# Issuing both transposes of a chunk ahead of their two copies

## The chip, the cores and the metric

The kernel runs on one core of a Trainium2 chip. The metric is the device time of one execution in microseconds (us); each kernel is run several times and the median is quoted. "Fast" runs are those in the chip's normal state, and only these are compared.

## The reference, cut to what matters

```python
# q, k, v: (8 batches, 8 heads, 576 positions, 64), float32
scores = scale * np.matmul(q, k.transpose(0, 1, 3, 2))
ret = scores * Dmat[None, :, :, :]            # causal, times gamma_h ** (i - j)
attn = np.matmul(ret, v)
x = attn.transpose(0, 2, 1, 3).reshape(4608, 512)
h = x @ w_in                                  # 512 -> 2048
g = h * np.tanh(softplus(h))                  # Mish
out = g @ w_out                               # 2048 -> 512
```

## The kernel before

The 4,608 rows are cut into chunks of 128, four chunks to a tile of 512. For each chunk, q and k are loaded, scaled by powers of gamma on VectorE (DVE), transposed on TensorE (PE) against an identity matrix into PSUM (the memory where this kernel's matmuls put their results), copied to SBUF (where it keeps its operands), and multiplied into scores. Masking and the product with v follow, then the two dense layers. The kernel fixes the order of PE's work by hand: pieces of attention for a later chunk are placed between groups of matmuls of the dense layers. A piece that waits holds back what stands behind it: in the prediction's timeline the 16 matmuls of L425, which need nothing from the transposes, start at 45.89, only after k's transposes, which had waited until 45.67.

The second tile (chunks 4 to 7) is transposed by `step_t`, the function that the change touches:

```python
def step_t(n):
    m, u = divmod(n, 2)
    qk = turned(m)                                              # SBUF tile "qkT" of a pair of chunks
    tp = ps_sc.tile([P, 4, NP, P], BF16, name="sc")             # PSUM; q in tp[:, 0], k in tp[:, 1]
    for i, copy in enumerate((nc.scalar.copy, nc.vector.tensor_copy)):
        flat = pairs[m]["qks"][:, i, u].rearrange("p h d -> p (h d)")
        for p in range(NP):                                     # NP = 4
            nc.tensor.transpose(tp[:, i, p, :], flat[:, ts(p, P)], ident)
        copy(qk[:, i, u], tp[:, i])
```

Around it stand the first dense layer with Mish on ScalarE (ACT), and the scores:

```python
def g1_chunk(n, f, nf=4):                                       # 16 matmuls of 128 columns
    ...
    nc.scalar.activation(gts[t][:, ds(f, nf), ts(s, P)], hp, AX.Mish)

def step_s(n):                                                  # needs both halves of qkT
    sc = ps_sc.tile([P, 2, NP, P], F32, name="sc")
    ... nc.tensor.matmul(sc[:, e, p, :], lhsT=qk[r, 1, u, p, :], rhs=qk[r, 0, u, p, :], ...)
    ... nc.vector.tensor_tensor(sm, sc, mask, op=OP.mult)

for n in range(4, 8):
    for fb in range(4):
        if n < 7:
            if fb == 0:
                one(n + 1, "T")                                 # step_t
            elif fb == 1:
                one(n + 1, "S")                                 # step_s
                ...
        g1_chunk(n, 4 * fb)
```

So from chunk 5 on one `g1_chunk` (16 matmuls) lies between a chunk's transposes and its scores. Chunk 4 is placed earlier, among the groups of the first tile, with two groups of four matmuls of 512 columns between.

## Time and profile before

| | before |
|---|---|
| median time | 321.31 us in the runs before the prediction, 321.19 with one more |
| PE busy | 305.4 us, 96% of the profiled span of 319.4 us |
| share of PE in the chain that ended last | 90% |
| PE idle before k's transposes, for ACT | 3.8 us, four times 0.94 |

A line of a timeline gives start and duration in us, engine, source line, operation, output and inputs, shapes and count, and in brackets the idle time of the engine before it with what ended that. PE's busy time contains a modelled pipeline tail after each last matmul (one short matmul is shown as 0.22 us though four in a row take 0.22), so an idle time in brackets is a little shorter than the hole in PE's stream. I therefore also use steps from one start to another. A view of a source line lists how long its engine sat idle before it and for whom.

### The profile page before, as it was taken

Reading aid. Unit: us, or ns where it says so; the run is one execution under the profiler, and the core shown is the slowest. Engines: PE = TensorE matmul, PEld = TensorE weight load, DVE = VectorE, ACT = ScalarE, POOL = GpSimd, SP = SyncE. Lnnn points to the kernel's source line nnn. Section 1 sums busy time; section 2 is a strip of 40 time slices with the busy share of each in tenths; the row PEclk is TensorE's granted clock in tenths of the full one; section 3 lists DMA queues with packets and bytes.
Section 4 is the critical chain, followed back from the end, with each engine's and each line's share of the span. In section 5 each row is a group of like instructions: output and inputs, shape, how many; then the busy total and the mean of one; then the engine's idle time right before and its main releaser. Section 6 shows DMA issues by size and latency. Waiting matters only on the chain.

```text
span 319.4 us, 6100 instructions
## 1 busy us (share of the span) xinstructions
PE 305.4 (96%) x2639; PEld 159.4 (50%) x2639; DVE 132.6 (42%) x178; ACT 129.6 (41%) x217; POOL 79.1 (25%) x102
## 2 busy tenths in 40 slices
PE   7788888999899999999999999999999999999995
PEld 2354477745555454444545454445454545444444
DVE  6733444047555675354444445353536232001111
ACT  5666566512464642243434343424242422333200
POOL 6687663551440040404131312140000000000000
PEclk9999999999999999999999999999999999999999
DMA  6999999999998549599795959595040400000032
GB/s 163 271 184 215 198 207 218 204 220 210 242 172 110 75 103 219 123 176 152 145 173 124 174 124 185 114 165 133 33 101 33 101 33 35 33 33 35 33 81 83
DMA packets 72474, 43.38 MB, mean 136 GB/s; under 512 B 55680, under 2 KB 63616, under 8 KB 72448
## 3 DMA queue, kind: packets, MB, share of 16 engines
q0 software_dynamic: 43952, 26.22, 55.8%
q1 hardware_dynamic: 28352, 16.65, 21.3%
q8 instruction: 20, 0.33, 0.5%
q10 hardware_dynamic: 144, 0.13, 0.1%
q14 instruction: 6, 0.05, 0.0%
HBM read 36.70 MB, written 9.44 MB: 144 GB/s over the span
## 4 chain that ended last, share of the span: by engine, by line
PE 90%; ACT 3%; SPq 2%; DMA 2%; DVE 1%; issue 1%; ACTq 0%; DVEq 0%
PE hp L402 34%; PE ops L440 32%; PE hp L440 6%; PE hp L425 5%; PE sc L338 3%; PE sc L387 2%; PE sc L380 2%; SPq L137 2%; PE st L359 2%; DMA kraw<-in_k_dram 2%; ACT qkT L310 1%; PE sc L309 1%; PE hp L452 1%; PE hp L413 1%; ACT qkT L297 1%
## 5 line engine op out<-in xcount | busy, mean ns | idle before, releaser
L402 PE MATMUL hp<-xT,w_in_t 128*128 128x512 bf16 x492 | 125.6, 380 | 0.5 <-ACT gT L427 0.5
L404 ACT ACTIVATE gT<-hp 128x512 bf16<-128x512 f32 x123 | 73.4, 597 | 128.6 <-PE hp L402 128.3
L440 PE MATMUL ops<-w_out_t,gT 128*128 128x512 bf16 x480 | 121.9, 379 | 0.0
L440 PEld LDWEIGHTS <-gT 128*128 128x128 bf16 x560 | 54.2, 98 | 64.7 <-issue 0.8
L460 DVE COPY res<-ops 128x512 f32<-128x512 f32 x30 | 20.7, 691 | 133.5 <-PE ops L440 133.5
L402 PEld LDWEIGHTS <-w_in_t 128*128 128x128 bf16 x492 | 45.6, 98 | 53.1 <-issue 0.8
L341 DVE TENSOR_TENSOR sm<-sc,mask 128x1024 bf16<-128x1024 f32 x36 | 42.6, 1217 | 13.6 <-PE sc L338 13.6
L318 POOL COPY seen<-qkT 1x1 bf16<-1x1 bf16 x10 | 1.8, 176 | 127.0 <-DMA qkT<-qks 127.0
L363 ACT ACTIVATE ssb<-st,diag 128x512 bf16<-128x512 f32 x32 | 20.2, 683 | 15.0 <-PE st L359 14.8
L107 POOL DMA_DIRECT2D qraw<-in_q_dram x16 | 17.2, 1074 | 24.7 <-DVE qks L280 18.5
L391 DVE CAST xT<-sc 128x512 bf16<-128x512 f32 x28 | 18.0, 685 | 4.7 <-PE sc L387 3.9
L280 DVE TENSOR_TENSOR qks<-kraw,gk 128x1024 bf16<-128x1024 f32 (+1 forms) x18 | 19.8, 1099 | 0.0
L280 DVE TENSOR_TENSOR qks<-qraw,gq 128x1024 bf16<-128x1024 f32 (+1 forms) x18 | 19.7, 1095 | 0.0
L440 PE MATMUL hp<-w_out_t,gT 128*128 128x512 bf16 x80 | 18.8, 380 | 0.0
L107 POOL DMA_DIRECT2D v<-in_v_dram x16 | 17.2, 1080 | 5.4 <-DMA kraw<-in_k_dram 2.7
L107 POOL DMA_DIRECT2D kraw<-in_k_dram x16 | 17.1, 1071 | 5.9 <-DVE qkT L297 3.7
L425 PE MATMUL hp<-xT,w_in_t 128*128 128x128 bf16 x276 | 17.1, 219 | 0.0
L425 PEld LDWEIGHTS <-w_in_t 128*128 128x128 bf16 x276 | 15.6, 98 | 0.7 <-issue 0.2
L387 PE MATMUL sc<-sm,v 128*64 128x128 bf16 x288 | 13.8, 220 | 0.6 <-DVE sm L341 0.6
L427 ACT ACTIVATE gT<-hp 128x512 bf16<-128x512 f32 (+1 forms) x18 | 10.3, 579 | 8.3 <-PE hp L425 8.1
L310 ACT COPY qkT<-sc 128x1024 bf16<-128x1024 bf16 x8 | 8.1, 1012 | 11.9 <-PE sc L309 11.9
L338 PEld LDWEIGHTS <-qkT 64*128 64x128 bf16 x288 | 8.1, 94 | 8.7 <-issue 6.4
(77 smaller groups left out, 163.2 us busy)
## 6 DMA issues: line engine op xcount, KB each, us to landing
out_dram<-res SPq DMA_DIRECT2D x31, 256.0 KB, 3.5
qraw<-in_q_dram POOLq DMA_DIRECT2D x12, 512.0 KB, 6.2
kraw<-in_k_dram POOLq DMA_DIRECT2D x12, 512.0 KB, 7.5
v<-in_v_dram POOLq DMA_DIRECT2D x12, 256.0 KB, 8.3
qraw<-in_q_dram POOLq DMA_DIRECT2D x8, 256.0 KB, 9.0
kraw<-in_k_dram POOLq DMA_DIRECT2D x8, 256.0 KB, 9.3
w_out_t<-in_moe_w_out_dram POOLq DMA_DIRECT2D x4, 512.0 KB, 12.1
w_in_t<-in_moe_w_in_dram POOLq DMA_DIRECT2D x6, 256.0 KB, 6.0
```

What stands on the lines that cost most here:

```text
L107: nc.gpsimd.dma_start(out=r[x][ds(off, ni)].rearrange("p u h d -> p (u h) d"), in_=src[ds(b, 2), :, ds(i0, ni), :].rearrange("b h p d -> p ...
L280: nc.vector.tensor_tensor(r["qks"][:, i, u], r["qk"[i]][:, u], g, op=OP.mult)
L338: nc.tensor.matmul(sc[:, e, p, :], lhsT=qk[r, 1, u, p, :], rhs=qk[r, 0, u, p, :], start=True, stop=True)
L341: nc.vector.tensor_tensor(sm.rearrange("p e n i -> p (e n) i"), sc.rearrange("p e n i -> p (e n) i"), (mask if len(chunks[n]) == 1 else ma ...
L363: nc.scalar.activation(ssb[:, :, :, e, :], st, AX.Copy, scale=diag[:, e:e + 1])
L387: nc.tensor.matmul(ot[ds(64 * e, 64), p, :], lhsT=vs[:, u, 2 * p + e, :], rhs=sm[:, e, p, :], start=(start and p == 0), stop=True, skip_gr ...
L391: (nc.scalar.copy if t < 2 else nc.vector.tensor_copy)(xts[t][:, :, ts(s, P)], ot)
L402: nc.tensor.matmul(hp, lhsT=w_in_t[:, c, ts(f, P)], rhs=xts[t][:, c, :], start=(c == 0), stop=(c == KC - 1))
L404: nc.scalar.activation(gts[t][:, f, :], hp, AX.Mish)
L425: nc.tensor.matmul(hp[:, j, :], lhsT=w_in_t[:, c, ts(f + j, P)], rhs=xts[t][:, c, ts(s, P)], start=(c == 0), stop=(c == KC - 1))
L440: nc.tensor.matmul(ops, lhsT=gts[t][:, f, ts(s, P)], rhs=w_out_t[:, f, :], start=(f == 0), stop=(f == nF - 1))
L460: copy(ot, ops)
```

## The change

The intent is to let PE issue all eight transposes of a chunk in a row and let the two copies follow, on ACT and DVE.

```diff
         tp = ps_sc.tile([P, 4, NP, P], BF16, name="sc")
-        for i, copy in enumerate((nc.scalar.copy, nc.vector.tensor_copy)):
+        for i in range(2):
             flat = pairs[m]["qks"][:, i, u].rearrange("p h d -> p (h d)")
             for p in range(NP):
                 nc.tensor.transpose(tp[:, i, p, :], flat[:, ts(p, P)], ident)
+        for i, copy in enumerate((nc.scalar.copy, nc.vector.tensor_copy)):
             copy(qk[:, i, u], tp[:, i])
```

## The prediction

> **What bounds the kernel now.** I read the page first: engine shares, slices, chain.
>
> ```profile
> PE 305.4 (96%) x2639; PEld 159.4 (50%) x2639; DVE 132.6 (42%) x178; ACT 129.6 (41%) x217; POOL 79.1 (25%) x102
> PE   7788888999899999999999999999999999999995
> PEclk9999999999999999999999999999999999999999
> PE 90%; ACT 3%; SPq 2%; DMA 2%; DVE 1%; issue 1%; ACTq 0%; DVEq 0%
> ```
>
> TensorE (PE) is busy 96% of the span at full clock, and 90% of the chain that ended last is its work. Only time taken from PE's stream, or from its idle time, shortens the kernel. The slices are 8 us wide; the ones with an 8 or less lie below 56 us, where the first two tiles are prepared. The second tile's chunks (4 to 7) are transposed there. So I asked next for the two source lines that the diff touches, the transposes (L296) and the copies (L297).
>
> ```profile
> L296 PE MATMUL sc<-ident,qks x32: 216/219/219, 30.8 to 52.1; 128*128 128x128 bf16 x32
>   ACT qkT L297: 3.8, 4
> L297 ACT COPY qkT<-sc x4: 580/580/581, 31.5 to 51.3; 128x512 bf16<-128x512 bf16 x4
> L297 DVE COPY qkT<-sc x4: 423/424/425, 32.6 to 52.4; 128x512 bf16<-128x512 bf16 x4
> ```
>
> Four chunks, eight transposes each, and PE sat idle four times, 3.8 us in all, until a ScalarE (ACT) copy ended. The timeline of one chunk (chunk 6) shows where. Columns: start, duration, engine, line, operation, idle before it and what ended that.
>
> ```profile
> 44.34 0.39 PE L296 MATMUL sc<-ident,qks 128*128 128x128 bf16 x4
> 44.54 0.60 ACT L427 ACTIVATE gT<-hp 128x512 bf16<-128x512 f32 x1 [0.41 <-PE hp L425]
> 45.04 0.58 ACT L297 COPY qkT<-sc 128x512 bf16<-128x512 bf16 x1
> 45.67 0.38 PE L296 MATMUL sc<-ident,qks 128*128 128x128 bf16 x4 [0.94 <-ACT qkT L297]
> 45.89 1.06 PE L425 MATMUL hp<-xT,w_in_t 128*128 128x128 bf16 x16
> 46.16 0.42 DVE L297 COPY qkT<-sc 128x512 bf16<-128x512 bf16 x1 [3.02 <-PE sc L296]
> 46.88 0.40 PE L338 MATMUL sc<-qkT 64*128 64x128 bf16 x8
> 47.32 1.22 DVE L341 TENSOR_TENSOR sm<-sc,mask 128x1024 bf16<-128x1024 f32 x1 [0.73 <-PE sc L338]
> ```
>
> The reader should see: q's four transposes, then nothing on PE until ACT has finished a Mish of the previous chunk (45.14) and q's copy (45.62), and only then k's four transposes, though they need nothing from q. The chain of waits runs through this very spot:
>
> ```profile
> 44.54 0.24 ACT gT L427
> 44.78 0.26 issue
> 45.04 0.59 ACT qkT L297
> 45.62 0.04 issue
> 45.67 0.38 PE sc L296 x4
> ```
>
> **What the Trainium skill says.** "PSUM — Partial Sum Buffer", section "PSUM bank collisions raise a hardware error": two different engines must not touch one bank and 32-partition quadrant at once, reads against reads included, and the compiler's scheduler orders every such pair, ScalarE against VectorE too. Both halves of this tile are 4 x 128 bf16 = 1,024 bytes per partition, together one 2 KiB bank of that page. The trace agrees: k's transposes start 0.05 us after q's copy ends, and the VectorE (DVE) copy of k never runs beside the ACT copy of q. The trace suggests that the framework is coarser still: in the later tiles one half fills 2,048 bytes, a bank of its own, and PE waits there too (L309 for the copies of L310).
>
> The same page, "Engine vs sequencer instructions": matmuls start and complete in program order. So a transpose that waits holds back the 16 matmuls of L425 behind it, which need neither copy; the 0.94 us idle above agrees.
>
> "Perfetto Trace Analysis", "Optimization Strategy": the same gap repeating on the engine that should be saturated is what to look for. Here it repeats four times at 0.94 us.
>
> **The change part by part.** No instruction is added or removed, and the built programs have the same order on every engine; only waits move. The list of waits in the two built programs says:
> 1. k's first transpose no longer waits for ACT. It was the cause of the bubble.
> 2. q's ACT copy waits for all eight transposes instead of four.
> 3. k's DVE copy waits for q's ACT copy, as before. Before, that was free, because k's transposes came later still; now it is the last thing before the scores (L338), which wait for it as they did.
> 4. The matmuls of L425/L402 and the scores get their own waits on ACT for older buffers, earlier met by way of the transposes. They name Mishes that ended long before.
>
> Gain of 1. Four transposes take 0.22 us of PE's stream (45.67 to the next instruction at 45.89). Without the wait, k's start at 44.34 + 0.22 = 44.56 instead of 45.67: 1.11 us sooner. (The idle of 0.94 is smaller since the view counts the modelled tail of the last matmul as busy.) The other chunks, by the same two rows: 30.77 and 32.09, 1.10; 37.74 and 39.07, 1.11; 50.57 and 51.90, 1.11. Sum 4.43 us.
>
> Cost of 2. In chunk 6 the eight transposes end at about 44.34 + 8 x 0.055 + 0.16 = 44.94; ACT is in its Mish until 45.14. Chunk 4: about 31.37 against a copy at 31.46. Nothing, or under 0.1 us.
>
> Cost of 3. ACT's copy of chunk 6 still ends at 45.62. ACT to DVE takes about 0.04 us (a DVE scaling at 4.39 follows an ACT end at 4.36; ACT to PE is 0.04 in the chain), the copy 0.42, DVE to PE 0.05 (a copy ends at 19.57, scores start at 19.62): scores can start at 45.62 + 0.04 + 0.42 + 0.05 = 46.13. PE gets there at 44.78 + 0.99 (the step from L425 to L338 before, 45.89 to 46.88) = 45.77 and so waits 0.36 us. The scores start 46.88 - 46.13 = 0.75 sooner, not 1.11. By the same sum, chunk 5: copy ends 39.02, scores 39.53 instead of 40.28, 0.75. Chunk 7: 51.85, 52.36 instead of 53.10, 0.74. In chunk 4 two full groups of matmuls (0.86 us each) lie before the scores at 34.13, which come at 33.03, while DVE is done at about 32.5: all 1.10.
>
> Sum: 1.10 + 0.75 + 0.75 + 0.74 = 3.34 us. After the scores, the masking on DVE (1.22) ends about 1.66 us after they start, and its reader comes 2.47 us after: no new wait.
>
> 321.31 - 3.34 = 317.97, rounded to 318.0, 1.0% less.
>
> **The rivals.**
> A: the whole 4.43 us, 316.9. It needs DVE to copy k beside ACT, or ACT to be quicker. Against it: the list of waits, and the order of the two copies that follows from it.
>
> B: the loads take the gain back, about 321. For it: DMA is over 90% busy up to 100 us. Against it: GpSimd's waits for older transfers tell when these landed, as each load waits for the one eight before it:
>
> ```profile
> 48.46 0.68 DVE L280 TENSOR_TENSOR qks<-qraw,gq 128x512 bf16<-128x512 f32 x1
> 55.31 1.15 POOL L107 DMA_DIRECT2D v<-in_v_dram  x1 [1.32 <-DMA kraw<-in_k_dram]
> 57.09 1.15 POOL L107 DMA_DIRECT2D qraw<-in_q_dram  x1 [0.63 <-DMA v<-in_v_dram]
> 65.01 1.21 DVE L280 TENSOR_TENSOR qks<-qraw,gq 128x1024 bf16<-128x1024 f32 x1
> ```
>
> The third tile's first q and k are in by 55.3 and 57.1 and are scaled from 65.01, or 61.7 when shifted: over 4 us of slack. Chunk 7's were in by 40.3 and are scaled at 48.46, or about 45.9. The last of the second weights can be dated by 52.8 (GpSimd's next wait); its first use moves from about 63.3 to 60. Later loads are spaced by DVE's use of the buffers and move along.
>
> C: the waits of part 4 or a late ACT copy cost something, making about 319. For it: ACT is the pacer at this spot. Against it: the Mish before the two in question ended 0.8 us earlier (43.57 in chunk 6).
>
> D: the time saved returns as idle time after 60 us. PE runs there at 9 tenths and more, paced by itself, so I give it little.
>
> **The range and the chances.** A sets the lower side and C the upper. The runs of before spread by 0.28 us. I take 317.2 to 319.1. A gain of over 2% needs 6.4 us, more than all four bubbles hold, so 0.01; a loss of 2% needs a new wait that nothing points to, 0.01; within 2%, 0.98.
>
> **What would show it.** Right: L296's idle for ACT gone; the eight transposes of a chunk 0.44 us apart in all; DVE's copy starting right after ACT's in chunks 5, 6 and 7; PE idle before L338 three times, some 0.2 to 0.4 us each, for DVE; the first L440 3.3 us earlier. Wrong: DVE's copy beside ACT's (then A), ACT's copy later relative to its Mish, idle of DVE for DMA at L280 (B), or a first L440 that is early with an end that is not (D).

## The result, and the profile after

The changed kernel took 317.89 us (median of 4 runs, 317.65 to 318.44) against 321.19 us before (320.99 to 321.34). The ratio is 0.990 with a 95% interval of 0.9883 to 0.9917; ratios here are the mean time of one kernel's fast runs over that of the other's in the same rounds, so not quite the ratio of the medians. That is 3.3 us, 1.0%.

The view of the transposes' line in the changed kernel:

```profile
L296 PE MATMUL sc<-ident,qks x32: 219/219/219, 30.6 to 48.2; 128*128 128x128 bf16 x32
its engine sat idle before it (us, times) until:
who waited for it (us, times):
```

(The first line of the view, on weight loads, is left out here and below.) Nothing stands under "sat idle" any more, where before it said 3.8 us for ACT. The timeline of chunk 6, to lay beside the one in the prediction (source lines from 297 on are one higher in this kernel, and ... marks lines left out):

```profile
42.31 0.61 PE L296 MATMUL sc<-ident,qks 128*128 128x128 bf16 x8
42.51 0.60 ACT L428 ACTIVATE gT<-hp 128x512 bf16<-128x512 f32 x1 [0.41 <-PE hp L426]
...
42.75 1.06 PE L426 MATMUL hp<-xT,w_in_t 128*128 128x128 bf16 x16
43.01 0.58 ACT L298 COPY qkT<-sc 128x512 bf16<-128x512 bf16 x1
...
43.63 0.42 DVE L298 COPY qkT<-sc 128x512 bf16<-128x512 bf16 x1 [2.52 <-ACT qkT L298]
...
44.11 0.40 PE L339 MATMUL sc<-qkT 64*128 64x128 bf16 x8 [0.30 <-DVE qkT L298]
```

The eight transposes run in one go, and the next group follows 0.44 us after their start. ACT's copy begins 0.70 us after the first transpose, exactly as before (45.04 against 44.34). What ends last now is the DVE copy: it waits for ACT's copy to end (43.59) and starts at 43.63, and then PE waits for DVE. The chain of waits shows the two copies end to end, and the summary of PE's waits (waiter, released by, us in total, times, longest) shows all three cases (chunks 5, 6 and 7):

```profile
43.01 0.59 ACT qkT L298
43.60 0.02 issue
43.63 0.43 DVE qkT L298
44.06 0.05 issue
44.11 0.40 PE sc L339 x8
```

```profile
PE sc L339 <- DVE qkT L298: 0.9, 3, 0.3
```

Was the time kept to the end? The traces start with loads from DRAM, and in the eleven sound traces the first transpose of chunk 4, ahead of which nothing differs, starts anywhere from 30.58 to 31.36 us. So I count from that start. The table gives, for each chunk, the step from its first transpose to its first score matmul, and from the first transpose of chunk 4 to the scores of chunk 7 and to the last matmul of the kernel.

| step, us | before | changed | gain | predicted |
|---|---|---|---|---|
| chunk 4, transpose to scores | 3.37 | 2.27 | 1.10 | 1.10 |
| chunk 5 | 2.54 | 1.79 | 0.75 | 0.75 |
| chunk 6 | 2.54 | 1.80 | 0.74 | 0.75 |
| chunk 7 | 2.53 | 1.79 | 0.74 | 0.74 |
| chunk 4's transpose to chunk 7's scores | 22.34 | 19.01 | 3.33 | 3.34 |
| ... to the last matmul of the kernel | 284.94 | 281.63 | 3.31 | 3.34 |

What is gained by 50 us is still there at the end. Do not read the gain off PE's busy time: it is 301.9 against 305.4 us, but with 2,602 recorded matmuls against 2,639, so 37 records are missing from the trace after. Experiment 4's trace of the same kernel has all 2,639 and shows 305.1 us: the gain came out of PE's idle time.

### The profile page after: what moved, and what is told of

Read it like the earlier page. It is cut to its first block, busy times and chain, and to the rows that moved or that the text cites. A ratio compares the mean times of both kernels' runs of the same rounds, so it can differ in the third digit from the quotient of the medians.

```text
span 315.9 us, 6059 instructions
## 1 busy us (share of the span) xinstructions
PE 301.9 (96%) x2602; PEld 158.9 (50%) x2639; DVE 132.6 (42%) x178; ACT 129.6 (41%) x217; POOL 78.6 (25%) x102
## 4 chain that ended last, share of the span: by engine, by line
PE 89%; ACT 3%; SPq 2%; DVE 2%; issue 2%; DMA 1%; ACTq 0%; DVEq 0%
PE hp L403 33%; PE ops L441 33%; PE hp L441 5%; PE hp L426 4%; PE sc L339 3%; PE sc L388 3%; PE sc L381 2%; SPq L137 2%; PE st L360 2%; DMA kraw<-in_k_dram 1%; ACT qkT L311 1%; PE sc L310 1%; PE hp L453 1%; PE hp L414 1%; ACT gT L428 1%
## 5 line engine op out<-in xcount | busy, mean ns | idle before, releaser
L403 PE MATMUL hp<-xT,w_in_t 128*128 128x512 bf16 x464 | 122.1, 380 | 1.4 <-ACT gT L428 0.5
L426 PE MATMUL hp<-xT,w_in_t 128*128 128x128 bf16 x276 | 17.1, 219 | 0.0
L426 PEld LDWEIGHTS <-w_in_t 128*128 128x128 bf16 x276 | 15.6, 98 | 0.7 <-issue 0.2
L339 PE MATMUL sc<-qkT 64*128 64x128 bf16 x288 | 11.9, 218 | 1.3 <-DVE qkT L298 0.9
```

The costliest lines, as they stand in the source:

```text
L403: nc.tensor.matmul(hp, lhsT=w_in_t[:, c, ts(f, P)], rhs=xts[t][:, c, :], start=(c == 0), stop=(c == KC - 1))
L426: nc.tensor.matmul(hp[:, j, :], lhsT=w_in_t[:, c, ts(f + j, P)], rhs=xts[t][:, c, ts(s, P)], start=(c == 0), stop=(c == KC - 1))
```

## The experiments

The theory has two halves. The bubble existed because k's transposes waited for ACT to finish reading the other half of the same PSUM tile. And the change gave 3.3 instead of 4.4 us because k's copy on DVE still waits for q's copy on ACT on that shared tile. The rivals: the order of instructions as such; sharing by bank instead of by tile; ACT's lateness instead of a second copy in a queue; an equal gain in every chunk; loads that take the gain back.

The kernels 1 to 4 ran on one chip and shared the runs of the kernel before; so did 5 to 8.

**1. Two tiles, old order.** The order of before, but k's half gets a PSUM tile of its own, from a pool that nothing else uses at that time.

```diff
-        tp = ps_sc.tile([P, 4, NP, P], BF16, name="sc")
+        tps = (ps_sc.tile([P, 4, NP, P], BF16, name="sc")[:, 0],
+               ps_o.tile([P, 2, NP, P], BF16, name="ops")[:, 0])
...
-                nc.tensor.transpose(tp[:, i, p, :], flat[:, ts(p, P)], ident)
-            copy(qk[:, i, u], tp[:, i])
+                nc.tensor.transpose(tps[i][:, p, :], flat[:, ts(p, P)], ident)
+            copy(qk[:, i, u], tps[i])
```

> The order of the kernel before (q's transposes, q's copy, k's transposes, k's copy), but k's transposes write to a PSUM tile of their own. Theory (the bubble comes from the two halves sharing a tile, not from the order): k's transposes wait for no ACT copy, DVE copies k beside ACT, the scores wait for neither; all four bubbles go in full, 1.10 + 1.11 + 1.11 + 1.11 = 4.43 us off the kernel before, about 316.8 us, 1.1 us under the changed kernel. Rival (the order as such matters): k's transposes still stand idle 0.94 us for ACT and the time stays at 321.2.

Measured: 316.64 us against 321.37, ratio 0.9855 (0.9842 to 0.9868). The timeline of chunk 6:

```profile
42.36 0.39 PE L296 MATMUL sc<-ident,qks 128*128 128x128 bf16 x4
...
42.58 0.39 PE L296 MATMUL ops<-ident,qks 128*128 128x128 bf16 x4
...
42.80 1.06 PE L425 MATMUL hp<-xT,w_in_t 128*128 128x128 bf16 x16
43.00 0.42 DVE L297 COPY qkT<-ops 128x512 bf16<-128x512 bf16 x1 [1.85 <-PE ops L296]
43.05 0.58 ACT L297 COPY qkT<-sc 128x512 bf16<-128x512 bf16 x1
...
43.79 0.40 PE L338 MATMUL sc<-qkT 64*128 64x128 bf16 x8
```

With the old order of instructions, k's transposes follow q's after 0.22 us, the two copies run side by side, and the scores start 1.44 us after the first transpose with no wait. From chunk 4's transpose to chunk 7's scores it is 17.94 us, 4.40 less than before (4.43 expected). So the order costs time only where the two halves share a tile; the reordering was a way around three quarters of that (3.33 of 4.40 us).

**2. One DVE copy.** The changed kernel, both halves copied by one DVE instruction.

```diff
-        for i, copy in enumerate((nc.scalar.copy, nc.vector.tensor_copy)):
-            copy(qk[:, i, u], tp[:, i])
+        nc.vector.tensor_copy(qk[:, :, u], tp[:, 0:2])
```

> The changed kernel with one DVE copy of both halves (1,024 elements per partition) in place of an ACT copy and a DVE copy behind it. Theory (what the change left is the DVE copy queued behind the ACT copy): in chunk 6 the copy starts some 0.1 us after the eight transposes (about 45.05 on the clock of the trace before), takes 0.69 us as the same copy does elsewhere, and the scores can start at about 45.79 where PE arrives at 45.77; nearly the full 4.43 us, 316.8 to 316.9 us. Rival (the 0.3 us waits before the scores cost nothing, or something else holds the scores): as the changed kernel, 317.9.

Measured: 316.97 us against 321.37, ratio 0.9863 (0.985 to 0.9877).

```profile
42.60 0.61 PE L296 MATMUL sc<-ident,qks 128*128 128x128 bf16 x8
...
43.05 1.06 PE L425 MATMUL hp<-xT,w_in_t 128*128 128x128 bf16 x16
43.25 0.69 DVE L297 COPY qkT<-sc 128x1024 bf16<-128x1024 bf16 x1 [1.85 <-PE sc L296]
...
44.04 0.40 PE L338 MATMUL sc<-qkT 64*128 64x128 bf16 x8
```

DVE is free at this moment and starts 0.65 us after the first transpose; one copy of twice the size takes 0.69 us where ACT's and DVE's one after the other took 0.58 and 0.42. It ends at 43.94 and PE arrives at 44.04. The step to chunk 7's scores is again 17.94 us. The remainder of 1.1 us (19.01 - 17.94) was thus the second copy in the queue, and there are two ways to be rid of it.

**3. Two banks of one tile, old order.** This puts to the test the Trainium skill's page "PSUM — Partial Sum Buffer", which in its section "PSUM bank collisions raise a hardware error" states the rule by bank and quadrant of 32 partitions (both halves here lie on all 128).

```diff
-                nc.tensor.transpose(tp[:, i, p, :], flat[:, ts(p, P)], ident)
-            copy(qk[:, i, u], tp[:, i])
+                nc.tensor.transpose(tp[:, 2 * i, p, :], flat[:, ts(p, P)], ident)
+            copy(qk[:, i, u], tp[:, 2 * i])
```

> The order of before and one PSUM tile as before, but k's half starts 2,048 bytes further on, in the next bank. Theory (the wait is kept by tile): the same waits as before, 0.94 us idle four times, 321.2 us. Rival (the wait is kept by bank, as the page on PSUM has it): k's transposes no longer wait, DVE copies beside ACT, as two tiles: 316.8 us.

Measured: 321.34 us against 321.37, ratio 0.9999 (0.9986 to 1.0011). From the view of the transposes' line:

```profile
L296 PE MATMUL sc<-ident,qks x32: 216/219/219, 31.4 to 52.7; 128*128 128x128 bf16 x32
...
  ACT qkT L297: 3.8, 4
```

PE waits for ACT four times, 3.8 us in all, as before. In this framework the wait is kept by tile: moving a half into another bank of the same tile changes nothing.

**4. The changed kernel again**, in the same rounds.

> The changed kernel itself, in the same rounds, to compare the others with: 317.9 us, 3.3 us under before.

Measured: 318.01 us against 321.37, ratio 0.9899 (0.9884 to 0.9914), with the steps of the first trace to 0.01 us except for the last matmul (281.70 instead of 281.63). The result repeats, and experiments 1 and 2 lie 1.4 and 1.0 us under it in the same rounds.

**5. The change for chunk 4 alone** (`if n == 4:` the new form, `else:` the old one).

> The change made for chunk 4 alone; chunks 5 to 7 keep the order of before. Theory (two full groups of matmuls lie before its scores, so the late DVE copy costs nothing there): the whole bubble, 1.10 us, comes off: 320.2 us, and no wait of the scores for DVE in this chunk. Rival (all four chunks gain alike, a quarter of 3.3): 0.83 us off, 320.5, with a wait of some 0.3 us before the scores of chunk 4.

Measured: 320.48 us against 321.21 over the fast runs, ratio 0.998 (0.9966 to 0.9993): 0.7 us, which fits the rival better. The profiled run could not decide: it took 801.58 us. From its page and the view of the second layer's line:

```profile
PE 793.0 (99%) x2639; PEld 299.6 (37%) x2639; DVE 134.4 (17%) x178; ACT 131.6 (16%) x217; POOL 78.7 (10%) x102
L448 PE MATMUL ops<-w_out_t,gT x480: 782/785/921, 121.3 to 776.6; 128*128 128x512 bf16 x160
```

Matmuls of 785 ns in the median instead of 379 (the steps from one to the next are mostly 621 ns instead of 216), the other engines about as busy as always, and no row of the granted clock on that page (the record lists a clock of 1.000 for this run, but its trace holds no clock event to show it). It looks like a state of that one execution, not of the kernel, whose other four runs lie within 320.43 to 320.75. So the kernel was run again.

> The change for chunk 4 alone once more, since the profiled run of the fifth experiment was an outlier of 802 us and its trace is of no use. As there: by the theory 1.10 us off (320.1 to 320.3) and no wait of the scores of chunk 4 for DVE; by the rival 0.83 us off (320.4 to 320.5) and a wait of some 0.3 us there. The step from the first transpose of chunk 4 to its scores is what tells: 3.37 us before, 2.27 by the theory, 2.54 by the rival.

Measured: 320.52 us against 321.30, ratio 0.9986 (0.9969 to 1.0003; one of six runs was 322.12). This trace is sound:

```profile
31.04 0.61 PE L297 MATMUL sc<-ident,qks 128*128 128x128 bf16 x8
...
33.31 0.40 PE L346 MATMUL sc<-qkT 64*128 64x128 bf16 x8
...
36.92 0.39 PE L304 MATMUL sc<-ident,qks 128*128 128x128 bf16 x4
...
38.24 0.38 PE L304 MATMUL sc<-ident,qks 128*128 128x128 bf16 x4 [0.94 <-ACT qkT L305]
...
39.14 0.42 DVE L305 COPY qkT<-sc 128x512 bf16<-128x512 bf16 x1 [2.96 <-PE sc L304]
...
39.62 0.40 PE L346 MATMUL sc<-qkT 64*128 64x128 bf16 x8
```

Chunk 4's own step is 33.31 - 31.04 = 2.27 us without a wait, as the theory says, 1.10 less than before. But chunk 5, in the old form here, takes 39.62 - 36.92 = 2.70 us instead of 2.54: its DVE copy begins 0.90 us after k's first transpose, against 0.49 in chunks 6 and 7 of the same run. That gives 0.16 back. The trace places the delay: the DVE queue's own semaphore instruction just before the copy runs at 38.67, as soon after k's first transpose (0.43 us) as in the other chunks, but the copy follows 0.47 us later, where elsewhere it is 0.06 to 0.07. ACT's copy, the other one it waits for, had ended at 38.19. From chunk 4's transpose to chunk 7's scores it is 21.40 us, 0.94 less than before, and the runs show 0.7 to 0.8.

I suspected a collision with GpSimd, which was issuing a load just then:

> One more look at the change for chunk 4 alone. In the last trace the DVE copy of chunk 5 (old order there) began 0.90 us after k's transposes began, against 0.49 in every other chunk of the old order, while GpSimd was issuing a load that had started 0.03 us before those transposes. If the two collide whenever they meet like this, the delay of 0.41 us and a step of 2.70 us for chunk 5 come again with the load at the same place; if GpSimd's load stands elsewhere this time, the step is 2.54. Chunk 4's own step is 2.27 either way.

Measured: 320.03 us against 321.50, one run each, of unknown state; only the trace is used. Chunk 5 took 2.70 us again, with GpSimd's issues elsewhere (one at 36.63, 1.15 us before k's transposes at 37.78, the next at 38.38). And in the kernel before, an issue that ran from 39.12 to 40.27 lay over the start of chunk 5's DVE copy (39.56) without delaying it. So it is not the coincidence of that load. The delay came in both sound traces of this build and in no other build, although the list of waits at this place is that of before. Its cause stays open.

**6. The change for chunks 5 to 7 alone.**

> The change made for chunks 5, 6 and 7 alone. Theory: 0.75 + 0.75 + 0.74 = 2.24 us off, 319.1 us, and three waits of some 0.3 us before the scores. Rival (alike): 2.5 us off, 318.9. The two times lie within the noise of each other; the trace's start of the scores against that of before is what tells.

Measured: 318.99 us against 321.21, ratio 0.9931 (0.9918 to 0.9943), 2.22 us. The times alone fit both views, as foreseen. The steps decide for the theory: 3.37 for chunk 4, then 1.79, 1.80 and 1.79, and 20.11 to chunk 7's scores, 2.23 less than before (2.24 expected). The two kinds of wait, before and after the change, stand in PE's waits of this one run, one bubble of the old kind and three rests of the new:

```profile
PE sc L304 <- ACT qkT L305: 0.9, 1, 0.9
PE sc L346 <- DVE qkT L299: 0.9, 3, 0.3
```

**7. The copies exchanged**, DVE first with q, ACT behind it with k.

```diff
-        for i, copy in enumerate((nc.scalar.copy, nc.vector.tensor_copy)):
-            copy(qk[:, i, u], tp[:, i])
+        nc.vector.tensor_copy(qk[:, 0, u], tp[:, 0])
+        nc.scalar.copy(qk[:, 1, u], tp[:, 1])
```

> The changed kernel with the copies exchanged: DVE takes q first, ACT takes k behind it. Theory (whichever comes second on the shared tile is late): DVE starts some 0.1 us after the eight transposes and is done at about 45.47 on the clock of the trace before, ACT, free of its Mish at 45.14, copies from 45.5 to 46.08, the scores start at about 46.13 as in the changed kernel: 317.9 us, with PE waiting before the scores for ACT now. Rival (the late copy is a matter of ACT being behind its Mish, which DVE is not): the scores find both halves in time, 316.8 us.

Measured: 317.93 us against 321.21, ratio 0.9897 (0.9884 to 0.9911), as the changed kernel.

```profile
43.35 0.42 DVE L297 COPY qkT<-sc 128x512 bf16<-128x512 bf16 x1 [1.85 <-PE sc L296]
43.86 0.59 ACT L298 COPY qkT<-sc 128x512 bf16<-128x512 bf16 x1 [0.36 <-DVE qkT L297]
...
44.51 0.40 PE L339 MATMUL sc<-qkT 64*128 64x128 bf16 x8 [0.30 <-ACT qkT L298]
```

Now ACT, idle for 0.36 us, waits for DVE, and PE for ACT. Whichever is second is late; ACT's Mish in front of its copy is not what costs the time (18.93 us from chunk 4's transpose to chunk 7's scores, against 19.01 in the changed kernel and 17.94 without the queue).

**8. Two tiles, and the pairs apart.** The same wait sits in the third and fourth tiles, where the two halves of a pair's transposes (L309) share a tile although each fills a bank. Here each gets its own tile, on top of experiment 1.

```diff
 def turn_pair(m, i):
-    if "tp" not in r:
-        r["tp"] = ps_sc.tile([P, 2, 2, NP, P], BF16, name="sc")
-    tp = r["tp"][:, i]
+    tp = ps_sc.tile([P, 2, 2, NP, P], BF16, name="sc")[:, 0]
```

> Two tiles for the second tile's chunks as in the first experiment, and in the third and fourth tiles also each half of a pair's transposes in a PSUM tile of its own. Theory (the same kind of wait, k's transposes for the ACT copy of q, sits there four times; by the trace before, k's transposes come 0.46, 1.03, 0.46 and 0.47 us later than PE could issue them, 2.4 us in all, and the ACT copies stay ahead of the scores): 316.7 - 2.4 = 314.3 us, 2.2% under before. Rivals: the copies now come too late for the scores there, which gives most of it back, 316 to 316.7; or loads from DRAM turn out the bound once PE is 7 us earlier, DVE waiting for DMA before it scales, 315 or more.

Measured: 314.38 us against 321.21, ratio 0.9787 (0.9774 to 0.98): 2.1% less. The interval reaches the line of 2% that separates "faster" from "same", so by that rule the verdict is unclear; that it takes less time than experiment 1 (0.9855) is clear. The line of these transposes in the kernel before, and then in this one:

```profile
  ACT qkT L310: 1.7, 4
```

```profile
L307 PE MATMUL sc<-ident,qks x64: 219/219/229, 64.9 to 101.0; 128*128 128x128 bf16 x64
its engine sat idle before it (us, times) until:
who waited for it (us, times):
```

From chunk 4's transpose to the last matmul it is 278.20 us, 2.36 less than in experiment 1 (280.56), where 2.4 was expected. In the list of DVE's waits the loads appear only before the first tile's scalings, so the loads are still not the bound with PE's last matmul 6.7 us earlier (278.20 against 284.94).

## Why the prediction was right

The predicted 318.0 us met 317.89, and each term of the sum can be checked. That the median lies within 0.11 us is partly luck, as single runs of the changed kernel lie anywhere from 317.65 to 318.44; the steps in the traces are the better test, and they show that the mechanism was right too.

- Gain of part 1: 1.10, 1.11, 1.11, 1.11 us for the four bubbles. Experiment 1, where nothing else hides it, has steps of 2.27 and three times 1.44 against 3.37, 2.54, 2.54 and 2.53: 1.10, 1.10, 1.10 and 1.09. Right to 0.02 us.
- Cost of part 2, ACT's copy waiting for all eight transposes: nothing. ACT starts 0.70 us after the first transpose before and after. Shown, but the margin was thinner than the prediction had it. It set the end of the transposes (44.94) against the end of ACT's Mish (45.14), while its own line has ACT's copy starting at 45.04; and in experiments 2 and 7 DVE, which waits for the same eight transposes and is free, starts 0.65 us after the first. That leaves some 0.05 us.
- Cost of part 3, DVE behind ACT: the prediction let PE wait 0.36 us in three chunks. The changed kernel's steps less those of experiment 1 are 1.79 - 1.44 = 0.35, 0.36 and 0.35. Experiments 2 and 7 show that this queue is the cause.
- Part 4, the new waits of the matmuls behind: L426 starts 0.44 us after the first transpose, right behind the eighth. No cost, so rival C is refuted by this and by part 2.
- Rival A (316.9) was what two tiles or one copy reach: 316.64 and 316.97. It was rejected for the right reason. Rivals B and D are refuted by the steps to the last matmul. Loads did not move forward with PE, though. In the changed kernel GpSimd's wait that ended at 56.53 says that the third tile's first q and k were in by then (55.31 before), and they were scaled from 61.49 and 62.62 (65.01 and 66.14 before): the slack is 5.0 us, about half of the 9.7 before. The prediction took its line at 57.09 for k; it names v, so its "over 4 us" was on the safe side.
- What the prediction said of the skill's page was too kind in one place: it let one bank explain the wait and only suspected a coarser rule. Experiment 3 shows the coarser rule. The sum did not rest on it, since it was made from the waits of the built program.
- Two readings were off. Not all slices with an 8 or less lie below 56 us: the one from 80 to 88 us is an 8 too (and the last a 5), and in it PE waits 0.84 us for an ACT copy before L309, the largest of the four waits that experiment 8 takes away. The prediction mentions L309's wait only in passing. Nor is it quite so that no instruction went: DVE's four semaphore instructions before its copies (L297) are gone with the waits. Neither touches its sum, which is about L296 alone.

Open remains why chunk 5's DVE copy was 0.41 us late in the build of experiment 5. And the difference of 0.3 us between experiments 1 and 2 is not explained by their traces, whose steps to chunk 7's scores are equal; starts scatter by more than that.

## What to carry to other kernels

Where two engines empty one PSUM tile in this framework, treat the tile as a resource that one engine holds at a time: the second copy queues behind the first, and a writer behind the copy placed before it. Here, reordering the writers left a shorter wait before the next reader (0.35 us in three of four chunks); separate tiles, or one copy by an engine that was free, removed it. To size such a change, take the step from the stalled instruction's start to where it could have started, and then follow the copies end to end to the instruction that reads both, as the second queue may now be the longest.

## What the Trainium skill lacked or had wrong

- "PSUM — Partial Sum Buffer", "PSUM bank collisions raise a hardware error", gives the rule by bank and quadrant. In this framework the wait was kept for the whole tile: halves in two banks of one tile still waited 0.94 us four times (ratio 0.9999), halves in two tiles not at all (0.9855).
- "Perfetto Trace Analysis", "Matmuls", advises to rotate matmul groups through different banks so that the emptying of one overlaps the next. Here that was not enough; they had to be different tiles (same two runs).
- I found no page with the time from the end of one compute engine's instruction to the start of the next one's within a kernel, which the sum needed: ACT to DVE 0.04 us (43.59 to 43.63), DVE to PE 0.05 us (44.06 to 44.11). Nearest is "Runtime: NRT & Kernel Launch", "The ~15µs preamble/postamble breakdown", with 44 ns per hop for the barrier before a kernel, which is about the same.
- "TensorE: Matmul & The Clock Gate", "What's actually happening", tells of a clock at half rate until PE has been busy some 3.4 us. One execution here had matmuls of 785 ns in the median instead of 379 and took 801.58 us with PE 99% busy, while the same kernel's other four runs took 320.43 to 320.75. That section does not account for it. A caveat further down that page tells of a clock seen stuck at a quarter for 50 us and more; the steps of 621 instead of 216 ns are 2.9 times as long, neither twice nor four times, so that stays open too.
- I found no page that explains a DVE copy that begins 0.41 us late in one build, in both of its sound traces, with the copies and transposes that it waits for done.
